# Which two slots of an attention stage carry no column block of the feed-forward matmul: third slots of a pair, or second ones

## The chip, the cores and the metric

One core of a Trainium2 chip runs the whole program. The metric is the device time of one execution in microseconds (us). The engines are named as in the profile: PE is TensorE, with PEld for its weight loads, DVE is VectorE, ACT is ScalarE, POOL is GpSimd, and SP is SyncE, which here only issues DMAs. Each engine takes its instructions in the order in which they stand in the program.

## The reference

Three layers follow each other: causal attention, a dense feed-forward layer, and a soft mixture of experts. Cut to what matters (q, k and v are 4 x 12 x 448 x 64, that is 4 batches of 12 heads; the middle layer is 768 to 2048 to 768 over 1792 tokens):

```python
scores = np.matmul(q, k.transpose(0, 1, 3, 2)) / np.sqrt(64)
attn = softmax(where(causal_mask, -1e9, scores))       # row maximum subtracted
x = (attn @ v).transpose(0, 2, 1, 3).reshape(1792, 768)
h = x @ w_in                                           # 768 -> 2048
g = np.maximum(0.01 * h, h)
x = g @ w_out                                          # 2048 -> 768
logits = x @ phi                                       # 32 slots, 4 for each of 8 experts
d, c = softmax(logits, axis=0), softmax(logits, axis=1)
slot_out[e] = np.maximum((d.T @ x)[e] @ w1[e], 0) @ w2[e]
out = c @ slot_out
```

## The kernel before, in words

Attention works on pairs of heads: there are 24, six for each batch. A generator, `attention_slots` (L506), hands out the work of a pair n in three slots. In the first slot PE multiplies the weights P of pair n-1 with v (tile O, from `attend`), transposes the maxima of pair n (mps), makes scores of pair n+1 for the row maxima (tile S_3, from `maxima`), and makes the first part of the transposed scores of pair n (T_0, from `weights`). The second slot makes the sums of pair n-1 (dn), the second part of the scores for the maxima (S_0) and T_1. The third slot turns pair n-1 into a piece of x16 (`columns`, no PE work from pair 6 on), and has T_2, S_1 and the eight transpositions of q and k of pair n+2 (qkps). So the names T_0, T_1, T_2 and S_3, S_0, S_1 say in which slot a tile stands.

ACT takes the exponential of every T (L397, to P); POOL clears the upper triangle of P (L401). DVE finds the maxima in every S by four instructions in the second slot (L361), and there it also takes two reciprocals of the sums (L439). The T and S tiles share two PSUM buffers, so that a T is written when the exponential of an older T, or the maxima of an older S, have been taken. H tiles have one PSUM buffer. Two buffers more (tag "tr") serve qkps, mps, dn and the small products.

The feed-forward layer is filled in between. The generator `up` (L585) gives for each of the 16 blocks of 128 columns of w_in one H of 18 matmuls, which take 3.5 us at full clock, followed by the activation g on ACT (L627). `stage` (L743) runs attention and `up` side by side: in slot x of 18 it issues the attention of the slot and then one H, except where x is in GAPS (L997), because there are 18 slots and 16 blocks. There are three such stages, for the batches 1, 2 and 3 of attention, beside `up(0)`, `up(1)` and `up(2)`. In the third, H is cut in two halves by the transposition of an older g (tile gps). A stage starts with the first slot of a pair, so that slots 8 and 17 are the third slots of the third and the sixth pair.

Also in between, in pieces that `prep_step` moves on after each slot, the weights w_in and w_out are converted from 64 to 32 bits: raw_i and raw_o are loaded, and ACT (L196, L197), DVE (L200, L201) and POOL (L216, L232) make cv_i and cv_o of them. PE has a part in it: w_ps, wt_ps, wp_ps and wf_ps. What stands with high priority (attention and `up`) keeps its order on PE by an explicit chain (L98); a scheduler places the rest around it.

After the stages, `up(3)` runs together with the logits of the older batches, while SP loads the experts' weights (w, L832) into buffers that become free.

Of the kernel before, what the change touches and what calls it, by code (L numbers as in the profile page):

```python
# [34 lines left out]
def tile_attn_moe_softmoe(ctx: ExitStack, tc: tile.TileContext, q, k, v, w_in, w_out, phi, w1, w2, out, dbg=None):  # L35
# [707 lines left out]
    def stage(slots, count, columns_of_g=None):  # L743

        had = started[0]
        for x in range(slots):
            with tc.high_priority(offset=AHEAD):
                next(slots_of_attention, None)
                if columns_of_g is not None and x not in GAPS:
                    next(columns_of_g)  # L750
# [243 lines left out]
NSPARE = 6  # L994
SPREAD = (1, 2)
VRING = 7
GAPS = (8, 17)  # L997


def tc_release(pool):  # L1000
# [31 lines left out]
```

## Time and profile before

| | |
|---|---|
| three timed runs | 711.86, 721.18, 721.48 us (median 721.18) |
| the profiled execution | 718.55 us; its span in the trace 716.8 us |
| busy: PE, DVE, ACT, POOL | 86%, 47%, 42%, 32% of the span |
| PE's H matmuls | 1152, busy 240.6 us |
| the three stages with GAPS | about 115 to 480 us from the span's start |

The profile lists the instructions of each engine in order of time, with the idle time ahead of each and the engine that ended it. Three timed runs lie up to 9.6 us apart, so a difference of a few microseconds between two executions says little.

### The profile page before, as it was taken

The page shows a single profiled execution, that of the slowest core. Times are in us where ns is not written, and L with a number is a line of the kernel's source. Part 1 is how long each engine was busy: PE and PEld are TensorE (multiplying, and loading weights), DVE is VectorE, ACT ScalarE, POOL GpSimd, SP SyncE. Part 2 cuts the span into 40 slices and gives each one's busy share as a digit, 9 for nine tenths or more (in the row PEclk, how much of TensorE's full clock was granted, in tenths as well). Part 3 has the DMA queues.
Part 4 walks back from the last instruction along what each step waited for, and adds up shares of the span by engine and source line. Part 5 has one row for each costly group of instructions (what it writes and reads, how often), then busy time and mean ns, then how long its engine had stood idle before and what let it go on. Part 6 is the DMA issues. An engine that isn't in the chain of part 4 may idle for free.

```text
span 716.8 us, 12198 instructions
## 1 busy us (share of the span) xinstructions
PE 616.6 (86%) x4764; PEld 350.0 (49%) x4764; DVE 338.9 (47%) x877; ACT 302.8 (42%) x596; POOL 231.5 (32%) x247
## 2 busy tenths in 40 slices
PE   3788859998978999899998999999999997984573
PEld 2455535554544555555555555554656553541121
DVE  5787645677875644563363555324334313010023
ACT  1677543566776545554445554422323220110012
POOL 4468733567765423442134442310000000000000
PEclk9799967999999999899999999999999999999877
DMA  9933154355345446422143222017759249999988
GB/s 196 250 95 78 39 173 139 109 166 152 102 157 197 122 132 206 134 84 74 53 127 115 67 67 68 23 52 276 262 198 333 83 177 350 408 400 399 393 287 270
DMA packets 117704, 125.66 MB, mean 175 GB/s; under 512 B 69520, under 2 KB 99216, under 8 KB 117648
## 3 DMA queue, kind: packets, MB, share of 16 engines
q1 hardware_dynamic: 117648, 124.90, 53.8%
q8 instruction: 37, 0.61, 0.3%
q14 instruction: 19, 0.16, 0.1%
HBM read 105.74 MB, written 19.14 MB: 174 GB/s over the span
## 4 chain that ended last, share of the span: by engine, by line
PE 55%; DMA 14%; DVE 12%; ACT 8%; POOL 3%; issue 3%; SPq 2%; DVEq 0%; ACTq 0%
PE H L100 24%; DMA w<-in_moe_w_dram 8%; PE O L100 6%; PE gps L100 4%; PE T L100 3%; DVE rs L439 2%; PE ph L897 2%; DMA v<-in_v_dram 2%; PE L L100 2%; PE pg L100 2%; DVE junk L361 2%; DMA raw_i_None<-in_moe_w_in_dram 2%; ACT mr L373 2%; PE qkps L100 2%; DMA raw_o<-in_moe_w_out_dram 2%
## 5 line engine op out<-in xcount | busy, mean ns | idle before, releaser
L100 PE MATMUL H<-x,w 128*128 128x448 f16 x1152 | 240.6, 354 | 1.5 <-ACT g L627 1.5
L100 PEld LDWEIGHTS <-w 128*128 128x128 f16 x1152 | 109.0, 98 | 103.7 <-issue 21.2
L361 DVE CUSTOM_DVE_ANT_0 junk<-S,mask 112x448 bf16<-112x448 f32 (+1 forms) x192 | 84.8, 442 | 74.5 <-PE S L100 72.0
L401 POOL TENSOR_SCALAR_AFFINE_SELECT P<-P 112x448 f32<-112x448 f32 x48 | 29.8, 621 | 144.3 <-ACT P L397 144.3
L627 ACT ACTIVATE g<-H,iv 128x448 f32<-128x448 f32 x58 | 36.6, 631 | 71.9 <-PE H L100 63.8
L397 ACT ACTIVATE P<-T 112x672 f32<-112x672 f32 (+1 forms) x72 | 57.0, 791 | 23.4 <-PE T L100 23.1
L100 PE MATMUL T<-qkt 64*112 64x336 f32 (+3 forms) x576 | 59.6, 319 | 6.1 <-ACT P L397 5.5
L100 PE MATMUL O<-P,v 112*64 112x448 f32 (+3 forms) x384 | 58.3, 449 | 5.0 <-POOL P L401 4.7
L439 DVE RECIPROCAL rs<-rs 128x224 f32<-128x224 f32 x36 | 53.3, 1521 | 12.6 <-ACT rs L437 12.6
L100 PEld LDWEIGHTS T<-qkt 64*112 64x112 f32 x576 | 45.4, 185 | 14.7 <-ACT P L397 6.9
L977 PE MATMUL po<-w,hz 128*32 128x384 f32 x256 | 30.3, 598 | 25.1 <-DMA w<-in_moe_w_dram 25.1
L410 POOL TENSOR_TENSOR tsum<-tsum,P 112x448 f32<-112x448 f32 (+1 forms) x48 | 44.8, 933 | 2.7
L100 PEld LDWEIGHTS O<-P,v 112*64 112x64 f32 x384 | 27.5, 150 | 34.8 <-issue 16.5
L373 ACT ACTIVATE mr<-mps,own 128x112 fp32r<-128x112 f32 x96 | 26.0, 354 | 43.2 <-PE mps L100 43.2
L570 DVE COPY g_nat<-gps 112x512 f32<-112x512 f32 x32 | 22.1, 689 | 44.1 <-PE gps L100 44.1
L568 ACT COPY g_nat<-gps 112x512 f32<-112x512 f32 x32 | 18.7, 584 | 54.3 <-PE gps L100 54.2
L406 POOL TENSOR_TENSOR tsum<-P 112x672 f32<-112x672 f32 x24 | 40.3, 1680 | 1.8
L100 PE MATMUL S<-qkt 64*112 64x448 f32 (+1 forms) x192 | 33.6, 391 | 7.1 <-DVE mxe L361 4.1
L100 PE MATMUL T<-mr,onesr 64*112 64x448 f32 (+1 forms) x192 | 32.0, 330 | 6.4 <-ACT mr L373 6.3
L890 POOL MEMSET hz<- 128x256 f32 x2 | 0.6, 311 | 112.8 <-PE pg L100 112.8
L216 POOL TENSOR_TENSOR cv_i_None<-cv_i_None,cs_i_None 128x768 f32<-128x768 f32 x16 | 26.8, 1681 | 28.6 <-ACT cs_i_None L215 28.5
L339 DVE TENSOR_TENSOR qkt<-qkps,qkt 128x448 fp32r<-128x448 f32 x48 | 28.1, 618 | 14.0 <-ACT qkt L338 14.0
(181 smaller groups left out, 898.8 us busy)
## 6 DMA issues: line engine op xcount, KB each, us to landing
w<-in_moe_w_dram SPq DMA_DIRECT2D x32, 1536.0 KB, 18.2
raw_i_None<-in_moe_w_in_dram SPq DMA_DIRECT2D x16, 768.0 KB, 5.9
raw_o_None<-in_moe_w_out_dram SPq DMA_DIRECT2D x10, 768.0 KB, 5.5
g_far<-g SPq DMA_DIRECT2D x32, 224.0 KB, 2.0
gb<-g_far SPq DMA_DIRECT2D x8, 896.0 KB, 8.5
wo<-wsc SPq DMA_DIRECT2D x4, 1536.0 KB, 6.4
qk<-in_q_dram SPq DMA_DIRECT2D x48, 112.0 KB, 2.6
qk<-in_k_dram SPq DMA_DIRECT2D x48, 112.0 KB, 2.9
```

The source lines that it names most:

```text
L100: op(*args, **kwargs)
L216: nc.gpsimd.tensor_tensor(t, t, sg, ALU.mult)
L339: nc.vector.tensor_tensor(st[:, j, 1], p, st[:, j, 0].bitcast(F32), ALU.subtract)
L361: nc.vector.tensor_tensor_reduce(out=junk[:, :w], in0=ps[:, a, at : at + w], in1=mask[:, S - w :], scale=-1.0, scalar=3e38, op0=ALU.add, o ...
L373: nc.scalar.activation(mr[:, i], ps, AF.Copy, scale=own[:, i : i + 1])
L397: nc.scalar.activation(x[:, :, o : o + at], ps[:, :, :at], AF.Exp, scale=SCALE)
L401: nc.gpsimd.affine_select(out=d, in_=d, compare_op=ALU.is_ge, fill=0.0, base=0, pattern=[[0, 4], [1, CP]], channel_multiplier=-1,)
L406: nc.gpsimd.tensor_tensor(tsum[:CP], p[0][:CP, :, 0, CP:], p[0][:CP, :, 1, : S - CP], ALU.add)
L410: nc.gpsimd.tensor_tensor(y, y, p[1][:CP, :, j, : S - CP * (j + 2)], ALU.add)
L439: nc.vector.reciprocal(rs[:, c : c + S // 2], rs[:, c : c + S // 2])
L627: nc.scalar.activation(g, ps, AF.Prelu, scale=iv[b][:, f : f + 1], alpha=SLOPE)
L977: nc.tensor.matmul(po[h][32 * g : 32 * g + 32], hp[:, (t0 + t) % 8], wt[:, t, DH * h - c0 : DH * (h + 1) - c0], start=t0 + t < 4, stop=t0 ...
```

## The change

One table changes: the slots of a stage that get no H.

```diff
-GAPS = (8, 17)
+GAPS = (7, 16)
```

Before, slots 8 and 17 had none. Now slots 7 and 16 have none, which are the second slots of the same pairs. Slot 7's block moves to slot 8, and slot 16's to slot 17; all other blocks stay. This makes six places. In the last of them (the end of the third stage) attention has no PE work left in the third slot, and the order on PE is as before. The other five are called A and B (first stage, pairs 9 and 12), C and D (second stage, pairs 15 and 18) and E (third stage, pair 21). In each, the H that stood between T_1 and T_2 now stands between qkps and O.

At C, PE's order was this before. In the names, T15_1 and T15_2 are the second and the third part of the transposed scores of pair 15, S16_1 is the last part of the scores of pair 16, qkps17 are the transpositions of pair 17; in brackets stand the semaphores that a row waits for.

```order
L100 MATMUL T15_1_3280<-mr15_3200,onesr_121 112x336 x2
L100 MATMUL H1_7_3292<-x16_1_1493,w16_1_99 128x448
...
L100 MATMUL wp_ps3_3314<-wt3_3247,phi_sb_93 32x128 [waits Activation_49]
L100 MATMUL wt_ps4_1_3329<-ident_64,cv_o4_None_3179 128x128 [waits Activation_49]
L100 MATMUL T15_2_3347<-qkt15_2859 112x224 x6
L100 MATMUL S16_1_3368<-qkt16_3122 112x224 [waits DVE_49]
L100 MATMUL qkps17_1_3383<-ident_64,qk17_2874 128x112 [waits DMAHW7_49,DMAHW6_49,Activation_49]
L100 MATMUL wf_ps3_3398<-istack_69,w4_3_3321 128x32 [waits DVE_49]
L100 MATMUL O15_3420<-P1_448_147,v15_2023 64x448 [waits Pool_49]
```

And this is the same place now.

```order
L100 MATMUL T15_1_3280<-mr15_3200,onesr_121 112x336 x2
L100 MATMUL wp_ps3_3292<-wt3_3247,phi_sb_93 32x128 [waits Activation_49]
L100 MATMUL wt_ps4_1_3307<-ident_64,cv_o4_None_3179 128x128 [waits Activation_49]
L100 MATMUL T15_2_3325<-qkt15_2859 112x224 x6
L100 MATMUL S16_1_3346<-qkt16_3122 112x224 [waits Activation_49]
L100 MATMUL qkps17_1_3361<-ident_64,qk17_2874 128x112 [waits DMAHW7_49,DMAHW6_49]
L100 MATMUL H1_7_3376<-x16_1_1493,w16_1_99 128x448
...
L100 MATMUL wf_ps3_3398<-istack_69,w4_3_3299 128x32 [waits DVE_49]
L100 MATMUL O15_3420<-P1_448_147,v15_2000 64x448 [waits Pool_49]
```

H1_7 moved from behind T15_1 to behind qkps17, and S16_1 now waits for ACT where it waited for DVE: it got the PSUM buffer of T15_2, and so waits for the exponential of T15_2 just ahead of it. This is so at B, C, D and E; at A it still waits for DVE, as before.

At B, where PE has nothing else between the two T, its order before was (T12 and mr12 belong to pair 12, S13 to pair 13):

```order
L100 MATMUL T12_1_2594<-mr12_2527,onesr_121 112x336 x2
L100 MATMUL H0_15_2607<-x16_0_500,w16_3_101 128x448 [waits Activation_49]
...
L100 MATMUL T12_2_2632<-qkt12_2232 112x224 [waits Activation_49]
L100 MATMUL S13_1_2653<-qkt13_2470 112x224 [waits DVE_49]
L100 MATMUL qkps14_0_2661<-ident_64,qk14_2247 128x112 [waits DMAHW6_49,DMAHW5_49]
L100 MATMUL O12_2694<-P0_448_145,v12_1314 64x448 [waits Pool_49]
```

Now it is:

```order
L100 MATMUL T12_1_2594<-mr12_2527,onesr_121 112x336 x2
L100 MATMUL T12_2_2609<-qkt12_2232 112x224 [waits Activation_49]
L100 MATMUL S13_1_2630<-qkt13_2470 112x224 [waits Activation_49]
L100 MATMUL qkps14_0_2638<-ident_64,qk14_2247 128x112 [waits DMAHW6_49,DMAHW5_49]
L100 MATMUL H0_15_2672<-x16_0_500,w16_3_101 128x448
...
L100 MATMUL O12_2694<-P0_448_145,v12_1314 64x448 [waits DVE_49,Pool_49]
```

T12_2 follows T12_1 at once, and waits for the exponential of T12_1, whose PSUM buffer it takes, as it did before with H0_15 in between.

At D, the order on ACT changes as well. Before (qkt20 is the copy of qkps20, mr19 the lowered maxima that PE needs for the last step of T_0 of pair 19, raw_o10 a block of w_out that is loaded at the start of the third stage):

```order
L338 CAST qkt20_4078<-qkps20_1_4086 128x448 [waits PE_49]
L373 ACTIVATE mr19_4134<-mps19_4132,own_124 128x112 [waits PE_49,Activation_49]
L397 ACTIVATE P1_448_147<-T19_0_4146 112x2x448 [waits PE_49]
L196 ACTIVATE cv_o10_0_4179<-raw_o10_0_4118 128x384 [waits DMAHW1_49]
L197 ACTIVATE cs_o10_0_4180<-raw_o10_0_4118 128x384
L196 ACTIVATE cv_o10_1_4250<-raw_o10_1_4120 128x384 [waits DMAHW2_49]
```

Now:

```order
L338 CAST qkt20_4056<-qkps20_1_4064 128x448 [waits PE_49]
L627 ACTIVATE g1_15_4107<-H1_15_4088,iv1_2727 128x448 [waits DMAHW5_49,PE_49]
L196 ACTIVATE cv_o10_0_4179<-raw_o10_0_4118 128x384 [waits DMAHW0_49]
L197 ACTIVATE cs_o10_0_4180<-raw_o10_0_4118 128x384
L196 ACTIVATE cv_o10_1_4250<-raw_o10_1_4120 128x384 [waits DMAHW1_49]
L373 ACTIVATE mr19_4134<-mps19_4132,own_124 128x112 [waits PE_49,Activation_49]
```

The conversions of raw_o10, which wait for its load, moved ahead of mr19.

## Rows read from the trace of the kernel before

**Rows 1.** The page: span, and busy time and instructions of each engine.

```profile
span 716.8 us, 12198 instructions
PE 616.6 (86%) x4764; PEld 350.0 (49%) x4764; DVE 338.9 (47%) x877; ACT 302.8 (42%) x596; POOL 231.5 (32%) x247
```

**Rows 2.** Waits of SP's queue: line waited for, us in total, times, longest.

```profile
SPq L832 <- PE H L100: 42.1, 4, 20.7
```

**Rows 3.** Timeline of PE, a regular pair; columns: start, us, instructions, count [idle before].

```profile
247.77 0.57 PE L100 MATMUL T<-qkt 64*112 64x224 f32 x6
...
249.79 3.57 PE L100 MATMUL H<-x,w 128*128 128x448 f16 x18
...
253.94 2.11 PE L100 MATMUL O<-P,v 112*64 112x448 f32 x16
...
257.86 3.58 PE L100 MATMUL H<-x,w 128*128 128x448 f16 x18
```

**Rows 4.** Timeline of PE at A: end of T_1, the wait, next H.

```profile
164.30 0.32 PE L100 MATMUL T<-mr,onesr 64*112 64x336 f32 x2
...
174.60 0.60 PE L111 MATMUL w_ps<-ident,w_am 128*128 128x128 f32 x2 [2.90 <-DVE qkt L339]
...
179.27 3.58 PE L100 MATMUL H<-x,w 128*128 128x448 f16 x18
```

**Rows 5.** Timeline of PE at C: end of T_1, the wait, O, next H.

```profile
287.77 0.32 PE L100 MATMUL T<-mr,onesr 64*112 64x336 f32 x2
...
297.66 0.61 PE L100 MATMUL wf_ps<-istack,w 96*128 96x32 f32 x2 [2.50 <-DVE qkt L339]
...
299.20 4.00 PE L100 MATMUL O<-P,v 112*64 112x448 f32 x16
...
305.18 3.58 PE L100 MATMUL H<-x,w 128*128 128x448 f16 x18
```

**Rows 6.** Timeline of PE at B: end of T_1, next H but one.

```profile
228.67 0.32 PE L100 MATMUL T<-mr,onesr 64*112 64x336 f32 x2
...
238.79 3.58 PE L100 MATMUL H<-x,w 128*128 128x448 f16 x18
```

**Rows 7.** Timeline of PE at D: end of T_1, next H but one.

```profile
356.52 0.32 PE L100 MATMUL T<-mr,onesr 64*112 64x336 f32 x2
...
366.68 3.58 PE L100 MATMUL H<-x,w 128*128 128x448 f16 x18
```

**Rows 8.** Timeline of PE at E: end of T_1, next H but one (first half).

```profile
420.61 0.32 PE L100 MATMUL T<-mr,onesr 64*112 64x336 f32 x2
...
433.34 1.88 PE L100 MATMUL H<-x,w 128*128 128x448 f16 x9
```

**Rows 9.** Timeline of ACT at A, B, C, D and E.

```profile
166.45 0.72 ACT L397 ACTIVATE P<-T 112x672 f32<-112x672 f32 x1
...
229.80 0.71 ACT L397 ACTIVATE P<-T 112x672 f32<-112x672 f32 x1
...
294.05 0.94 ACT L196 ACTIVATE cv_o_None<-raw_o_None 128x768 f32<-128x768 f32 x1
...
365.15 1.09 ACT L373 ACTIVATE mr<-mps,own 128x112 fp32r<-128x112 f32 x4 [2.03 <-PE mps L100]
...
369.94 0.55 ACT L196 ACTIVATE cv_o<-raw_o 128x384 f32<-128x384 f32 x1 [2.04 <-DMA raw_o<-in_moe_w_out_dram]
...
423.90 0.55 ACT L197 ACTIVATE cs_o<-raw_o 128x384 bf16<-128x384 f32 x1 [2.21 <-DMA raw_o<-in_moe_w_out_dram]
```

**Rows 10.** Three stretches: length, busy us of each engine, granted clock, DMA.

```profile
211.00:216.00 5.00, 2.88 (x20) 1.93 (x21) 4.93 (x15) 2.86 (x6) 4.11 (x3) 1.00 0.39 142
298.00:304.00 6.00, 6.00 (x33) 3.06 (x34) 0.13 (x1) 1.62 (x5) 2.56 (x3) 0.50 0.51 149
376.00:384.00 8.00, 6.37 (x44) 4.09 (x43) 4.63 (x16) 4.98 (x10) 5.67 (x6) 0.79 0.42 119
```

## The prediction

> **What bounds the kernel now.** I read the page first: PE is busy 616.6 us of a span of 716.8 us, and no other engine more than 49% [rows 1]. So in the stages PE is the engine to follow, and a microsecond in which PE stands still there is one that the end gets. It reaches the end undiminished: the weights of the experts are loaded when PE's last H tiles have freed their buffers (SP's queue waits for PE's H 42.1 us in four waits [rows 2]), so that the tail, where DMA is the bound, starts when PE gets there.
>
> Then I read PE's timeline at the five places, always from the end of T_1 to the H that follows O, because between these two points the change moves one H and nothing leaves. The reader is to see what each neighbour of H hides. Before, the two old waits in slot 8 stand out: at A PE waits 2.90 us [rows 4] and at C 2.50 us [rows 5], both behind qkps, for DVE's copy of qkt, because the small product after qkps needs the buffer that DVE still reads. [...] At B, D and E PE has no such wait, or a short one.
>
> **The change, part by part.** Nothing is added or removed: the same instructions run, one H of 3.5 us moves in each of five places. What it covered is laid open, and what stands behind it now is covered.
>
> *What is laid open.* T_2 takes the PSUM buffer of T_1, so it cannot start before ACT has taken the exponential of T_1. Before, H ran in that time. S_1 waits at B, C, D and E for the exponential of T_2 right ahead of it, a wait that did not exist. An exponential takes 0.71 to 0.72 us [rows 9] once ACT comes to it; T_2 itself has about 0.9 us.
>
> *What is covered.* The 3.5 us of H now lie over DVE's copies of qkt and over POOL's work on P. The waits at A and C should be gone.
>
> *Unit for the sum.* In a regular pair T_2 to H is 2.02 us, H to the next is 3.5, and O to the H after it is 3.92 (257.86 - 253.94) [rows 3]; together 9.4 us at full clock. Each place then is: its waits, its small products, and 9.4.
>
> A. Before: 164.62 to 179.27, 14.65 us [rows 4]. ACT ended the exponential of T_1 at 166.45 + 0.72 = 167.17, since conversions of w_in stood ahead of it [rows 9]. So T_2 starts 2.6 us late. S_1 waits for DVE's maxima, which come behind its reciprocals: between nothing and 0.9 us (the price of the new wait at the other places), I take 0.45. With two w_ps of 0.35 each: 2.6 + 0.45 + 9.4 + 0.7 = 13.15. Gain 1.5 us.
>
> C. Before: 288.09 to 305.18, 17.1 us [rows 5]. Now wp_ps and wt_ps stand between T_1 and T_2, 1.6 us of work which covers the exponential. Behind T_2, ACT has a conversion of 0.94 us [rows 9] to do ahead of the exponential, so S_1 waits 1.2 us. Then wf_ps and wp_ps, 0.8: 1.6 + 1.2 + 9.4 + 0.8 = 13.0. Gain 4.1 us, of which the clock is the larger part: O to H took 5.98 us there [rows 5] instead of 3.92.
>
> B. Before: 228.99 to 238.79, 9.8 us [rows 6]. The exponential of T_1 started at 229.80 [rows 9], behind a conversion that had waited for its load; it ends at 230.51, so T_2 is 1.6 us late. S_1 waits 0.9 for its exponential. With one v_ps of 0.3: 1.6 + 0.9 + 9.4 + 0.3 = 12.2. Loss 2.4 us.
>
> D. Before: 356.84 to 366.68, 9.84 us [rows 7]. The same pair of waits, with ACT taken as idle: 0.65 and 0.85; 1.5 + 9.4 + 0.4 = 11.3, loss 1.5 us. But on ACT four conversions of raw_o10 now stand ahead of mr19, without which PE cannot end T_0 of pair 19. They started at 369.94, when the load had landed [rows 9]. The loads follow the transpositions qkps20, which now end some 1.85 us earlier (3.5 us of H gone, 1.5 us of waits and handing over come), so the conversions start between 368.1 and 369.9 and need 1.9 us (four of nearly 0.5); mr19 takes 1.09 [rows 9], and H follows 0.4 later: 371.5 to 373.3 instead of the 368.1 without the block. The loss is thus 1.5 us at least (load early, no block) and 6.6 at most; I take 4. Something comes back: before, the same loads held up PE in the first slots of the third stage, 1.6 us of idle time and a mean clock of 0.79 in 376 to 384 [rows 10], which is 1.6 + 8 x 0.21 = 3.3 us. With the loads early and PE late these should mostly go; I take 3 of them. D comes to a loss of 1.
>
> E. Before: 420.93 to 433.34, 12.4 us [rows 8]. T_2 waits 0.3 behind wp_ps. The exponential of T_2 stands on ACT behind a conversion that ran at 423.90, when its load landed, to 424.45 [rows 9]. T_2 ends at about 422.6, so S_1 starts only at 425.2, 2.55 us late. With gps, wf_ps and wt_ps: 0.6 + 0.3 + 2.55 + 9.4 + 1.1 = 13.95. Loss 1.5 us.
>
> Sum at full clock: +1.5 + 4.1 - 2.4 - 1 - 1.5 = 0.7 us gained.
>
> *The clock.* It is the term that the trace leaves open. After 2.50 us of idle PE at C the granted clock fell; after 2.1 us of idle (5.00 - 2.88) at 211 to 216 it stayed at 1.00 [rows 10]; in 376 to 384 1.6 us in two pieces let it fall. A fall costs between 1.7 us (8 x 0.21 [rows 10]) and 2.8 us (at C: 2.06 from O to H, and 0.7 in the small products ahead of O [rows 5, 3]). New idle times are 3.05 at A, 2.5 at B, 1.2 at C, 1.5 or more at D, 2.85 at E, each in two pieces close together. I count two falls of 1.7: 3.4 us, though none or four are as well possible.
>
> [...]
>
> Forecast: -0.7 + 3.4 = 2.7 us slower. On the profiled execution, 718.55 us, that is 721.3. The median of the three runs, 721.18, lies 2.6 us above that execution, and the lowest, 711.86, lies 6.7 below; I set 722 us for the median, between 721.3 and 723.9.
>
> **The rivals.**
>
> 1. *The new waits are hidden.* ACT could come to the exponentials earlier, because g has left its place ahead of them; then T_2 and S_1 wait only 0.7 each. For it: at D and E g did stand in that stretch. Against: at A and B what stood ahead were conversions and their loads, which stay. Priced: A, B and E gain another 1.5 us each, no clock falls: -0.7 - 4.5 = 5 us faster, 713.3 on the profiled execution, 716 by the median.
>
> [...]
>
> 3. *Slower by more: D's block without the return.* ACT stands on the load of raw_o10 while PE runs out of work, its loads are not earlier, and the old holdup in 376 to 384 stays: loss of 6.6 at D in place of 1, with a fall of the clock of 2.8 and two more falls of 1.7. The sum is -0.7 + 5.6 + 6.2 = 11 us, 730 to 733 us; it becomes more than 2% (14.4 us) only if the gain at C fails too, 735 us and more. It decides once the conversions start after 369.9.
>
> 4. *Nothing moves where it matters.* At the sixth place the order on PE is the same, so nothing changes there; for the other five the order shows the move, which leaves this rival no room of its own.
>
> **How the numbers follow.** Forecast within 5 us of 722: 0.6. Rival 1: 0.17. Rival 2: 0.13. Rival 3: 0.1, of which 0.03 go beyond 2%. The likeliest is 722. Low: rival 1 on an execution like the lowest of the three would be 707; leaving that out, 712 takes in its 716 and the spread below. High: 731, which takes in most of rival 2. So 712 to 731 us; the forecast's own range is 717 to 727. What a measurement of this kernel can tell from no change is about 2%, 14.4 us: faster 0.02, same 0.94, slower 0.04.
>
> **What would show it.** In the profile after: no wait for DVE's qkt of more than 1 us behind qkps at A and C, with the clock at 1.00 in the 10 us behind C, and O of 2.1 us there; T_2 waits for ACT's P at A and B by more than 1 us; S_1 waits for ACT's P at B, C, D, E by 0.8 to 2.6 us; mr19 late at D, with PE waiting for it, and no wait for wt in the slots after it. The total is wrong if the clock falls at none or at all of the places, or if the conversions, whose loads run on their own time, meet the exponentials otherwise than in this one execution. C is the largest single term: if its wait only moves to another place, the change is slower by 6 us or more.

## The result and the profile after

The changed kernel takes 728.66 us (median of four runs, 725.35 to 734.95), the kernel before 719.49 us beside it (four runs, 711.86 to 721.48). The ratio is 1.0147, with a 95% interval of 1.0098 to 1.0196, so the change costs 10.6 us (7 to 14). The forecast was a loss of 2.7 us, 722 us, with a range of 712 to 731: the sign was right and the size a quarter of what came. The time lies outside the forecast's own range (717 to 727), and inside the stated one only because that made room for rival 2, a clock fall at each of A, B, D and E (729 to 732), just below which it ended.

The page of the kernel after: span, busy time of each engine, and the granted clock in 40 equal slices, in tenths.

```profile
span 733.2 us, 12197 instructions
PE 623.5 (85%) x4764; PEld 353.7 (48%) x4764; DVE 344.7 (47%) x877; ACT 302.4 (41%) x596; POOL 231.7 (32%) x247
PEclk9999977998988799999999999999999998999787
```

The engines do the same work as before [rows 1]; PE is busy 6.9 us longer and idle 9.5 us longer. Ahead of a T it waits 11.5 us in all for ACT's P (5.5 before), ahead of an S 10.1 us for DVE's maxima (4.1 before). What the stages lose reaches the end, as the prediction assumed: the last O starts 15.4 us later (488.88 against 473.52), and the span is 16.4 us longer.

PE's timeline after shows the end of T_1, the waits and the H matmuls at the five places and, ahead of B, in pair 11 (columns as in [rows 3]). The first four rows are of A (before: [rows 4]), the next two of pair 11, then five of B ([rows 6]), four of C ([rows 5]), five of D ([rows 7]) and four of E ([rows 8]).

```profile
166.02 0.32 PE L100 MATMUL T<-mr,onesr 64*112 64x336 f32 x2
168.84 0.90 PE L100 MATMUL T<-qkt 64*112 64x224 f32 x6 [2.51 <-ACT P L397]
172.34 5.12 PE L100 MATMUL H<-x,w 128*128 128x448 f16 x18
181.75 0.55 PE L100 MATMUL H<-x,w 128*128 128x448 f16 x2
...
219.08 0.53 PE L100 MATMUL S<-qkt 64*112 64x224 f32 x2 [4.28 <-DVE mxe L361]
221.09 4.65 PE L100 MATMUL H<-x,w 128*128 128x448 f16 x18
...
234.82 0.32 PE L100 MATMUL T<-mr,onesr 64*112 64x336 f32 x2
238.77 0.91 PE L100 MATMUL T<-qkt 64*112 64x224 f32 x6 [3.64 <-ACT P L397]
241.34 0.53 PE L100 MATMUL S<-qkt 64*112 64x224 f32 x2 [0.82 <-ACT P L397]
243.34 5.46 PE L100 MATMUL H<-x,w 128*128 128x448 f16 x18
252.98 3.58 PE L100 MATMUL H<-x,w 128*128 128x448 f16 x18
...
301.97 0.32 PE L100 MATMUL T<-mr,onesr 64*112 64x336 f32 x2
305.82 0.36 PE L100 MATMUL S<-qkt 64*112 64x224 f32 x2 [1.04 <-ACT P L397]
311.66 0.41 PE L100 MATMUL wf_ps<-istack,w 96*128 96x32 f32 x2 [1.16 <-DVE qkt L339]
316.68 3.58 PE L100 MATMUL H<-x,w 128*128 128x448 f16 x18
...
368.01 0.32 PE L100 MATMUL T<-mr,onesr 64*112 64x336 f32 x2
369.15 0.56 PE L100 MATMUL T<-qkt 64*112 64x224 f32 x6 [0.49 <-ACT P L397]
370.99 0.36 PE L100 MATMUL S<-qkt 64*112 64x224 f32 x2 [0.82 <-ACT P L397]
381.58 0.45 PE L100 MATMUL T<-mr,onesr 64*112 64x448 f32 x2 [2.36 <-ACT mr L373]
381.97 3.58 PE L100 MATMUL H<-x,w 128*128 128x448 f16 x18
...
433.04 0.32 PE L100 MATMUL T<-mr,onesr 64*112 64x336 f32 x2
437.58 0.36 PE L100 MATMUL S<-qkt 64*112 64x224 f32 x2 [2.38 <-ACT P L397]
439.03 3.20 PE L100 MATMUL H<-x,w 128*128 128x448 f16 x9
448.73 1.88 PE L100 MATMUL H<-x,w 128*128 128x448 f16 x9
```

Nearly every wait that the prediction named is there (only S_1 at A has none): T_2 and S_1 wait for ACT's P, and an H of 3.6 us behind such a wait takes up to 5.46 us. From the end of T_1 to the H behind O, A takes 15.41 us (before 14.65), B 17.84 (9.8), C 14.39 (17.1), D 13.64 (9.84), E 15.37 (12.4). The windows (length, busy time of PE, PEld, DVE, ACT, POOL, then the granted clock, DMA) show where the clock fell:

```profile
170.00:182.00 12.00, 12.00 (x69) 6.94 (x68) 8.55 (x18) 5.70 (x13) 7.49 (x6) 0.77 0.67 197
236.00:249.00 13.00, 9.41 (x46) 5.80 (x48) 5.87 (x15) 3.91 (x7) 5.51 (x6) 0.61 0.21 57
300.00:318.00 18.00, 15.49 (x133) 9.20 (x132) 12.62 (x26) 11.31 (x23) 9.74 (x8) 1.00 0.50 152
368.00:384.00 16.00, 12.33 (x92) 7.17 (x89) 10.40 (x30) 8.16 (x18) 7.48 (x8) 1.00 0.49 137
436.00:446.00 10.00, 8.42 (x45) 5.07 (x47) 4.64 (x15) 4.23 (x9) 3.85 (x5) 0.83 0.03 12
```

These are A, B, C, D and E: the clock fell at A, B and E, and stayed at 1.00 at C and D. It fell in pair 11 too, twice: H took 5.21 us in its first slot (at 202.86; the clock was 0.76 in 202 to 209) and 4.65 in its third (the row at 221.09; 0.65 in 217 to 226).

One stretch that the prediction did not look at lost time as well. Against the profile of before, O of pair 10 starts 2.5 us later (196.47 against 193.98), and O of pair 11 7.9 us later (225.67 against 217.74): 5.4 us are lost in between, where the change moves nothing on PE.

### The profile page after: what moved, and what is told of

It reads as the page before. It is cut to its first block, busy times and chain, and to the rows that moved or that the text cites. A ratio compares the mean times of both kernels' runs of the same rounds, so it can differ in the third digit from the quotient of the medians.

```text
span 733.2 us, 12197 instructions
## 1 busy us (share of the span) xinstructions
PE 623.5 (85%) x4764; PEld 353.7 (48%) x4764; DVE 344.7 (47%) x877; ACT 302.4 (41%) x596; POOL 231.7 (32%) x247
## 5 line engine op out<-in xcount | busy, mean ns | idle before, releaser
L100 PE MATMUL H<-x,w 128*128 128x448 f16 x1152 | 246.8, 361 | 1.3 <-ACT g L627 1.3
L100 PEld LDWEIGHTS <-w 128*128 128x128 f16 x1152 | 111.3, 100 | 106.6 <-issue 27.0
L100 PE MATMUL T<-qkt 64*112 64x336 f32 (+3 forms) x576 | 60.3, 322 | 12.2 <-ACT P L397 11.5
L100 PE MATMUL O<-P,v 112*64 112x448 f32 (+3 forms) x384 | 53.7, 422 | 5.1 <-POOL P L401 4.7
L410 POOL TENSOR_TENSOR tsum<-tsum,P 112x448 f32<-112x448 f32 (+1 forms) x48 | 46.7, 972 | 2.2
L100 PE MATMUL S<-qkt 64*112 64x448 f32 (+1 forms) x192 | 33.4, 388 | 15.7 <-DVE mxe L361 10.1
L100 PEld LDWEIGHTS O<-P,v 112*64 112x64 f32 x384 | 26.1, 141 | 33.2 <-issue 16.4
L406 POOL TENSOR_TENSOR tsum<-P 112x672 f32<-112x672 f32 x24 | 39.8, 1660 | 1.7
```

The costliest lines, as they stand in the source:

```text
L100: op(*args, **kwargs)
L406: nc.gpsimd.tensor_tensor(tsum[:CP], p[0][:CP, :, 0, CP:], p[0][:CP, :, 1, : S - CP], ALU.add)
L410: nc.gpsimd.tensor_tensor(y, y, p[1][:CP, :, j, : S - CP * (j + 2)], ALU.add)
```

## The experiments

The theory was that each place costs its new buffer waits and the clock fall behind them, and that the rest (pair 11, and B's T_2 wait of 3.64) follows from A. The rivals were a clock fall at every moved place alike, and spread between executions. The kernels run the same instructions in another order; e6_b_raw4 and e7_raw4 have one buffer more, and e8_b_fill adds matmuls that nothing reads.

**Parts of the change.** GAPS becomes a table by stage, `x not in GAPS[b]`:

```diff
-GAPS = (8, 17)
+GAPS = (7, 17)                                  # e1_pair1: A, C, E
+GAPS = (8, 16)                                  # e2_pair2: B, D
+GAPS = {1: (7, 16), 2: (8, 17), 3: (8, 17)}     # e3_stage1: A, B
+GAPS = {1: (8, 17), 2: (7, 17), 3: (8, 17)}     # e4_c_alone: C
+GAPS = {1: (8, 16), 2: (8, 17), 3: (8, 17)}     # e5_b_alone: B
```

> Only the first of the two slots moves (7, 17): places A (stage 1), C (stage 2) and E (stage 3). Theory (each place costs what its new buffer waits and the clock fall behind them cost, as the trace of the changed kernel shows it place by place): A -0.8, C +2.7, E -3.0, so 1 us slower than before, within 0.5%. Rival 1 (the 5.4 us lost between A and B is a knock-on of A): 6 to 7 us slower, 0.9%, and the stretch between H_8 and H_15 shows it again. Rival 2 (every moved place costs a clock fall of 1.7 us and nothing else): 5 us slower at all three places alike.

> Only the second of the two slots moves (8, 16): places B (stage 1) and D (stage 2). Theory: B -6.3 and D -0.9, 7 us slower than before, 1.0%, with a wait of T_2 of over 3 us and a clock of 0.50 at B. Rival 1 (B lost so much only because the pairs ahead of it were late and a load of w_in then stood ahead of the exponential on ScalarE): B costs 2 to 3 us, the kernel is 3 to 4 us slower. Rival 2 (a clock fall of 1.7 us at each place): 3.4 us slower.

> Stage 1 alone gets the new slots (places A and B). Theory: A -0.8, the stretch between A and B -5.4, B -6.3: 12 us slower than before, more than the whole change cost by its median (9.2), since C gives 2.7 back. Rival 1 (the stretch between A and B is spread between executions): 7 us slower. Rival 2 (two clock falls): 3.4 us slower.

> Place C alone (first slot of stage 2). Theory: the wait of 2.50 us and the slow matrix products behind it go, a wait of S_1 of about 1.0 us comes: 2.7 us faster than before, 0.4%, and faster than both kernels. Rival (a moved place costs a clock fall wherever it is): 1.7 us slower.

> Place B alone (second slot of pair 12 in stage 1). Theory: B is where the change loses most, and loses more than the 2.4 us of the sum: 6 to 7 us slower than before (0.9%), of which e2_pair2 showed 4.9 in its trace and the changed kernel 6.3. T_2 waits over 1 us for ACT's P, and the granted clock falls to 0.50 in the H behind. Rival 1 (the prediction's own price, 2.4 and a clock fall of 1.7): 4.1 us slower. Rival 2 (D carries the loss of e2_pair2): within 2 us of before.

| | ratio to before, 95% interval | us |
|---|---|---|
| e1_pair1 (A, C, E) | 1.0024 [0.9997, 1.0051] | +1.7 |
| e2_pair2 (B, D) | 1.0121 [1.0083, 1.0159] | +8.7 |
| e3_stage1 (A, B) | 1.0108 [1.0064, 1.0151] | +7.8 |
| e4_c_alone (C) | 0.9982 [0.9955, 1.0008] | -1.3 |
| e5_b_alone (B) | 1.0068 [1.0039, 1.0098] | +4.9 |

The us are the ratio less 1, times 720; each is uncertain by 2 to 3 us either way, and a difference of two of them by 3 to 4. The parts add up: e1_pair1 and e2_pair2 give 10.4, the whole change 10.6. B costs 4.9, D the other 3.8 of e2_pair2. C gives 1.3, half of what the theory had from one trace, and its interval includes nothing as well as the 2.7 of the theory. A and E with pair 11 cost about 3 together (1.7 + 1.3). That a moved place costs one fall of 1.7 us wherever it is, falls with e2_pair2 (8.7 where it said 3.4) and e4_c_alone. The theory missed as well: e3_stage1 costs 7.8 where it said 12, e5_b_alone 4.9 where it said 6 to 7 (the prediction's own price, 4.1, fits too), and the loss of e2_pair2 is not 6.3 at B and 0.9 at D, as the next table shows.

The traces say more, place by place. (The profiled execution of e3_stage1 was the longest of its six, 736.64 us.) The table gives the us from the start of T_1 to the first H behind O (for pair 11 from O of pair 10 to its own O), each from two rows of PE's timeline; a star marks a place with the new slot.

| | A | pair 11 | B | C | D | pair 19, behind D | E |
|---|---|---|---|---|---|---|---|
| before | 15.43 | 23.76 | 10.58 | 17.87 | 10.63 | 18.51 | 13.20 |
| e10_before_again | 16.80 | 24.11 | 10.58 | 17.88 | 10.64 | 16.85 | 13.20 |
| after | 16.19* | 29.20 | 18.63* | 15.17* | 14.42* | 15.63 | 16.15* |
| e11_after_again | 16.71* | 29.56 | 18.93* | 15.18* | 14.72* | 15.59 | 16.27* |
| e1_pair1 | 17.00* | 28.90 | 12.19 | 15.16* | 10.62 | 16.27 | 16.03* |
| e2_pair2 | 15.29 | 23.51 | 13.97* | 15.35 | 14.44* | 15.94 | 13.19 |
| e3_stage1 | 16.89* | 31.64 | 16.71* | 17.86 | 10.63 | 18.49 | 14.89 |
| e4_c_alone | 16.84 | 23.51 | 10.58 | 15.47* | 10.63 | 16.15 | 13.19 |
| e5_b_alone | 16.53 | 24.32 | 14.09* | 15.34 | 10.63 | 16.77 | 13.20 |
| e6_b_raw4 | 14.59 | 24.33 | 14.42* | 17.85 | 10.63 | 16.01 | 13.20 |
| e7_raw4 | 16.25 | 24.35 | 10.94 | 15.36 | 10.63 | 16.47 | 13.20 |
| e8_b_fill | 15.77 | 24.34 | 13.99* | 17.87 | 10.62 | 16.77 | 17.01 |

D and E cost about 3.8 and 2.9 wherever they are moved, and D nothing where it is not; E, unmoved, loses 1.7 us in e3_stage1 by the clock alone (O takes 3.80 us) and 3.8 in e8_b_fill, for which see below. B costs 3.4 to 3.8 with A unmoved, and 6.1 to 8.4 with A moved; even unmoved, behind a moved A, it loses 1.6 (e1_pair1). Pair 11 loses 4.5 us and more in each of the four traces with A moved, and in none of the eight others. C is the surprise: left as it was, it takes 17.9 us in some traces and 15.4 in others.

**The clock at C.** The next rows are of PE at C in e2_pair2, then in e6_b_raw4; in neither does the change touch C.

```profile
305.37 0.41 PE L100 MATMUL wf_ps<-istack,w 96*128 96x32 f32 x2 [2.50 <-DVE qkt L339]
306.46 2.11 PE L100 MATMUL O<-P,v 112*64 112x448 f32 x16
```

```profile
301.29 0.63 PE L100 MATMUL wf_ps<-istack,w 96*128 96x32 f32 x2 [2.49 <-DVE qkt L339]
302.86 4.00 PE L100 MATMUL O<-P,v 112*64 112x448 f32 x16
```

The wait is the same, and the work ahead of it too. In one O takes 2.11 us, in the other 4.00. Of the eight traces with C unmoved, e2_pair2, e5_b_alone and e7_raw4 kept the clock (O 2.11 us in each); before (twice), e3_stage1, e6_b_raw4 and e8_b_fill lost it (4.00 in each). So 2.5 of the 2.7 us that the trace of the changed kernel gains at C are the clock (17.87 against 15.34 to 15.36 with C unmoved), and are there to be gained only in an execution in which it had fallen behind the wait.

**Both kernels once more**, nothing edited.

> The kernel before, profiled once more, nothing changed. Theory (the clock falls after one and the same wait in one execution and not in another): the places A to E wait as in the first profile, 2.9 at A, 2.5 at C and none over 0.5 at B and D, but the stretch at C can take 15.4 instead of 17.9 us, the one behind D 16 to 17 instead of 18.5, and the first slot of pair 12 can lose the clock where it did not. Rival (the clock follows from the program): every stretch within 0.3 us of the first profile.

> The changed kernel, profiled once more, nothing changed. Theory: the waits come again (T_2 2.5 to 3.7 at A and over 1 at B, S_1 0.8 at B and D, 2.4 at E), B with A moved ahead of it takes 16 to 19 us where B alone took 14.1, D 14.4, E 16.1; only the stretches of pair 11 and A vary, by 1 to 2 us, as the clock falls or not. Rival (the loss between A and B of the first profile was an accident of that execution): pair 11 takes no longer than in the kernel before.

In the kernel before, C lost the clock again (17.88), which the theory had left open; behind D the stretch took 16.85 in place of 18.51, and pair 12 kept the clock (H 3.58 us at 226.43). So it is not the program alone that decides, but the two traces agree in more than I expected. In the changed kernel pair 11 took 29.56, so its loss is no accident. S_1 there waited 5.95 us for DVE, and T_2 at B 3.93 us for ACT.

Here one program shows both outcomes of the clock. Behind the same two waits for qkt, of 0.8 and 1.4 us, the H in the first slot of pair 11 took 5.21 us in the first profile and 3.58 in the second (at 202.96). The pair is no shorter for it: S_1 waits 1.7 us longer for DVE and starts at the same time (219.22 against 219.08). So a clock fall ahead of a longer wait cost nothing here.

**What B costs: the load, or the two exponentials?** Four buffers for the loaded blocks, with B alone and without it.

```diff
-    BUFS = ((3, 4, 2), (3, 3, 2), (2, 2, 2))
+    BUFS = ((3, 4, 2), (4, 3, 2), (2, 2, 2))
```

> B alone, and four buffers instead of three for the loaded blocks of w_in and w_out in the first two stages with H, so that the block of w_out that ACT converts ahead of the exponential of T_1 at B can be loaded earlier. To be compared with e7_raw4. Theory (the load, which ACT waits for ahead of the exponential, makes B dear): at B no wait of ACT for raw_o ahead of the exponential, T_2 waits under 1.5 us, and this is 2.5 to 4 us slower than e7_raw4. Rival (two exponentials in a row and the clock fall alone make B dear, whenever the load comes): 6 to 7 us slower than e7_raw4.

> The kernel before with four buffers for the loaded blocks instead of three, to compare e6_b_raw4 with. Theory: loads come earlier, and the waits of ACT for raw blocks that hold up mr or the exponentials in stages 1 and 2 get shorter: 1 to 4 us faster than before. Rival (the loads are bound by the conversions that free the buffers): same within 1 us.

e7_raw4 has a ratio of 1.0002 (0.9977 to 1.0027), e6_b_raw4 one of 1.0015 (0.9986 to 1.0044). The difference is 0.9 us with some 2.8 either way: the rival's price of 6 to 7 is out, but what makes up B's cost the times don't tell. The traces do for the place: with the load taken earlier (no conversion stands between g and the exponential any more), T_2 still waits 1.32 and S_1 0.83 us, and B takes 3.5 us more than in e7_raw4, as in e5_b_alone against before. So in its place B alone does not cost what it costs because of the load; two exponentials in a row and the clock do it. By the times B costs 0.9 us with four buffers and 4.9 with three, 4.0 apart with some 3.5 either way; where the rest went is open. PE at B in e5_b_alone:

```profile
235.25 0.57 PE L100 MATMUL T<-qkt 64*112 64x224 f32 x6 [0.99 <-ACT P L397]
237.09 0.49 PE L100 MATMUL S<-qkt 64*112 64x224 f32 x2 [0.82 <-ACT P L397]
239.06 4.33 PE L100 MATMUL H<-x,w 128*128 128x448 f16 x18
```

T_2 to H takes 3.81 us, of which 0.82 are the wait and 2.02 the work at full clock [rows 3]; the 0.97 left and the 0.75 that H takes beyond 3.58 are the clock: 1.7 us.

**Filling the waits.** B alone, with matmuls that nothing reads in the place of the waits.

```diff
+    def fill(count):
+        ps = psum.tile([128, S], F32, tag="H", bufs=HB[0], name=f"fill{count}")
+        for step in range(count):
+            mm(ps, w16[3][:, 0, 0, :128], x16[0][:, 0, 0, :], start=step == 0, stop=step == count - 1)
...
                 weights(n, 1)
+            if n == 12:
+                fill(9)
             yield
...
                 weights(n, 2)
+            if n == 12:
+                fill(4)
```

> B alone, with 9 extra matmuls of H's kind (1.8 us) into H's free buffer between T_1 and T_2, and 4 (0.8 us) between T_2 and S_1; nothing reads their results. They only keep PE at work while it would wait. Theory (the fall of the clock is a good part of what B costs): the H of slot 17 takes 3.6 us instead of 4.2 to 5.5, the granted clock stays at 1.00, and in spite of 2.6 us more work the kernel is 1 to 2.5 us faster than e5_b_alone. Rival (the waits themselves are the whole cost): no faster than e5_b_alone, up to 1 us slower.

PE at B in e8_b_fill:

```profile
233.15 1.88 PE L100 MATMUL fill<-x,w 128*128 128x448 f16 x9
235.90 0.93 PE L100 MATMUL fill<-x,w 128*128 128x448 f16 x4
...
238.67 3.57 PE L100 MATMUL H<-x,w 128*128 128x448 f16 x18
```

And a window over B in e5_b_alone, then in e8_b_fill:

```profile
233.00:243.00 10.00, 8.19 (x57) 5.36 (x56) 6.69 (x17) 4.30 (x7) 5.50 (x6) 0.83 0.26 69
```

```profile
232.00:242.00 10.00, 9.27 (x71) 5.48 (x69) 6.79 (x17) 4.10 (x7) 5.56 (x6) 1.00 0.24 64
```

The clock stays at 1.00, H takes 3.57 us, and 2.8 us of extra work cost nothing in the place: B takes 13.99 us, with e5_b_alone at 14.09. So by these two traces the fall at B comes with PE standing still there, and its size, half of B's cost, fits; that filling makes the kernel faster does not hold. The kernel as a whole took 1.0166 (1.0127 to 1.0205), 7 us more than e5_b_alone. In its trace 2.5 us are the clock at C (17.87 against 15.34), and the larger loss is at E, which the edit was not to touch: 17.01 us in place of 13.20, with a wait of PE for mr of 3.75 us and a clock fall behind it. What changed there is the order on ACT, as at D: a conversion of raw_o that waits for its load stands ahead of mr. ACT at E in e8_b_fill:

```profile
440.81 0.54 ACT L197 ACTIVATE cs_o<-raw_o 128x384 bf16<-128x384 f32 x1 [4.42 <-DMA raw_o<-in_moe_w_out_dram]
441.26 1.06 ACT L373 ACTIVATE mr<-mps,own 128x112 fp32r<-128x112 f32 x4
```

In the kernel before mr ran first (431.81), and the conversion behind it (435.03); there and in e5_b_alone PE waited under 0.2 us for mr. So the fill at B cost its gain by a new order somewhere else.

**The first slots.** What if the slot without H is one whose H covers little?

```diff
-GAPS = (8, 17)
+GAPS = (6, 15)     # e9_first
+GAPS = (6, 17)     # e12_first_third
```

> The first slots of the same pairs carry no H (6, 15). Then the H between T_1 and T_2 stays, and one stands between qkps and O too; what is laid open is the exponential of T_0 (0.92 us), over which the dn products and S_0 (1.6 us in the kernel before, pair 9) run. Theory (a slot is worth what its H covers): T_1 waits for nothing or under 0.5 us, no place costs more than 0.5 us, the waits for DVE's qkt of 2.90 at A and 2.50 at C go, with the clock falls behind them where they came: 3 to 7 us faster than before, 0.4 to 1.0%. Rival (any slot without H lays a wait open and brings a clock fall): 5 to 10 us slower, like the changed kernel.

> In each stage the first slot of the third pair and, as in the kernel before, the third slot of the sixth pair carry no H (6, 17). By the traces the first slot is cheap at A, C and E, while at B and D the third slot is the cheapest: with no H in the first slot of pair 18 (15) e9_first waited 2.19 us for mr there, behind the conversions of raw_o10, and took 64.0 us from O of pair 17 to O of pair 20 where kernels with D as before took 61.3 to 63.7. Theory: the gains of e9_first at A and C stay, its losses at B (0.7) and D (0.3 to 2.7) go: 5 to 8 us faster than before, 0.7 to 1.1%, and 1 to 3 us faster than e9_first. Rival (the gains of e9_first come from the second of its slots): no faster than before.

e9_first takes 718.78 us (ratio 0.9939, 0.9911 to 0.9968; 4.4 us faster), e12_first_third 712.82 us (0.9882, 0.9838 to 0.9926; 8.5 us faster than before). The first time came as expected (3 to 7; at D it still waits 2.19 us for mr), the second a little beyond its range (5 to 8), and both kernels beat the two compared here. Windows over A and C in e12_first_third:

```profile
159.00:174.00 15.00, 12.58 (x92) 7.09 (x92) 12.20 (x35) 10.64 (x17) 9.52 (x8) 1.00 0.44 115
289.00:299.00 10.00, 9.53 (x80) 5.75 (x77) 4.88 (x16) 6.88 (x16) 5.70 (x6) 1.00 0.83 260
```

No wait for qkt of 2.9 or 2.5 us is left at A and C, as H stands behind qkps there, and H also stands between T_1 and T_2. What is laid open, the exponential of T_0, costs under 0.5 us, because dn and S_0 run over it. A still has 2.11 us of waiting (S_1 for DVE's maxima), without a fall of the clock. Against the first trace of before the gain lies at C, 4.8 us (2.5 of them the clock that this trace had lost), in pairs 9 to 11 together, 2.4 (pair 10 loses 3.6 by a wait of S_1 and a clock fall, pair 11 gains 4.4), and behind D, 2.3; E gains nothing.

## Why the prediction came out as it did

**The waits at the places: right.** T_2 waits 2.51 us at A (2.6 in the sum), 0.49 at D (0.65), 0.26 at E (0.3); S_1 waits 1.04 at C (1.2), 0.82 at B and D (0.9, 0.85), 2.38 at E (2.55). Three did not come so: S_1 at A has no wait (0.45 in the sum), T_2 at B waits 3.64 us (1.6; 0.99 with B alone), and wf_ps at C still 1.16 (nothing). At D the conversions of raw_o10 stand ahead of mr19 as the order said. ACT at D, after:

```profile
378.55 0.55 ACT L196 ACTIVATE cv_o<-raw_o 128x384 f32<-128x384 f32 x1 [2.21 <-DMA raw_o<-in_moe_w_out_dram]
...
380.47 1.07 ACT L373 ACTIVATE mr<-mps,own 128x112 fp32r<-128x112 f32 x4
```

PE waits 2.36 us for mr, and D loses 3.8 us, where I took 4 between bounds of 1.5 and 6.6. That it came so close is in part luck: with T_1 at D 11.49 us later than before (368.01 against 356.52), the conversions started 1.0 us ahead of the earliest time that the sum had allowed (378.55 - 11.49 is 367.06, not 368.1). From 368.1 the sum gives a loss of 4.8, from 367.06 the 3.8 that came. So rival 1 (waits hidden) and rival 3 (conversions after 369.9) are both out.

**The clock: the number of falls was wrong.** I counted two falls of 1.7 us. It fell at A, B and E: 3.0 us at A (T_2 to H is 3.50 in place of 2.02, and H to O 5.05 in place of 3.5), 1.7 at B alone and 3.6 with A moved (T_2 to H 3.75 without the wait, and H 5.46), 1.7 at E (3.20 for half an H in place of 1.88, and qkps 1.38 in place of 0.99). At full clock A would have gained the 1.5 us of the sum and 0.7 more; with the fall it lost 0.8 (and in other traces A unmoved takes from 14.6 to 16.8 us where the first took 15.4, by the clock and by a wait of H for g of up to 1.7 us). These falls, 8.3 us in place of 3.4, are, with the 5.4 us of pair 11 below, the largest parts of the miss in the trace. Rival 2's term, four falls at up to 2.8 us each, no run shows: the traces have three, at A, B and E, of 3.0, 3.6 and 1.7 us, while D waited 0.49, 0.82 and 2.36 us with the clock at 1.00. That the total came out near its 10.5 us is therefore partly luck: it had nothing in pair 11.

**Three returns were booked against one execution.** At A the sum gave a gain of 1.5 us. But the trace of before had lost the clock there too, behind the wait of 2.90 us, which the prediction did not see:

```profile
174.00:180.00 6.00, 5.40 (x27) 3.19 (x28) 4.70 (x14) 1.71 (x5) 1.94 (x3) 0.72 0.58 169
```

That is 1.7 us (6 x 0.28), so the gain is no more than that execution's own loss; behind the same wait (2.90 and 2.91 us) e2_pair2 and e6_b_raw4 kept the clock (O's second part 0.79 us, 1.39 in that trace). At C I took 4.1 us, the larger part for the clock that the first trace had lost there; in three of the eight traces with C unmoved it had not been lost. The wait did not go away either: S_1's 1.04 came as priced, but wf_ps still waits 1.16 us for DVE's qkt, behind H, which the sum had at nothing. C alone gives 1.3 us by the times (between a loss of 0.6 and a gain of 3.2), 2.4 by its trace against both of before; how often the kernel before loses the clock at C is open, since both of its traces did. At D I took 3 of 3.3 us back from the slots behind it. In the profile of before these took 18.51 us, and 15.63 after, so by that trace the 3 came; but in the other traces with D unmoved they take 16.0 to 16.9, except e3_stage1 (18.49). D as a whole cost 3.8 us by the times, not 1.

**Pair 11 was not looked at: the queue that was moved past.** The loss there follows A (four traces of four, none of eight without). Two things changed. First, S_1 of pair 11 now gets the PSUM buffer of S_0, and so waits for DVE's maxima; before, it had that of T_2 and waited for ACT, 2.24 us. Second, SP's queue is in another order: the load of v for pair 17 comes behind two blocks of w_out instead of between them. SP after (start, us, instruction, count; the second issue waits within the 4.80 us):

```profile
198.47 4.80 SPq L173 DMA_DIRECT2D raw_o_None<-in_moe_w_out_dram  x2
...
204.38 0.38 SPq L311 DMA_DIRECT2D v<-in_v_dram  x1
```

The same place in e10_before_again:

```profile
198.07 0.35 SPq L173 DMA_DIRECT2D raw_o_None<-in_moe_w_out_dram  x1
...
198.99 0.38 SPq L311 DMA_DIRECT2D v<-in_v_dram  x1
204.73 0.33 SPq L173 DMA_DIRECT2D raw_o_None<-in_moe_w_out_dram  x1
```

DVE after: its instruction for that v stands ahead of the maxima of S_0 that PE waits for, and a conversion too.

```profile
209.53 0.69 DVE L324 TENSOR_REDUCE v_am<-v 112x1 f32<-112x512 f32 x1 [3.49 <-DMA v<-in_v_dram]
...
214.33 2.92 DVE L200 TENSOR_SCALAR cv_o_None<-cv_o_None 128x768 int32<-128x768 int32 x1
```

Both changes stand in the order of the program; the prediction followed PE and ACT and left SP, DVE and the pairs between the places out. Which of them costs how much wasn't tried. An estimate: in e10_before_again, where O of pair 10 starts 0.1 us later, DVE had done with these maxima at 217.98 and S_1, waiting for ACT, started at 216.10; in the changed kernel it started at 219.08. So of some 3.1 us the buffer by itself would make 1.9 and the late maxima the rest; the clock fall behind S_1 adds 2.0 (qkps 1.75 us, H 4.65). In e12_first_third, with the S_0 buffer and the old order of SP, v was reduced at 201.51 and pair 11 has no such wait; but there DVE takes the maxima ahead of a conversion as well, so this is no clean test.

**What B costs beside A.** At B the sum had 2.4 us, and 4.1 with a fall. B alone cost 4.9 us by the times, 3.5 in its trace: right in size. With A moved its T_2 waits 3.64 us, since ACT waits for a block of w_out ahead of the exponential. ACT after:

```profile
237.22 0.88 ACT L197 ACTIVATE cs_o_None<-raw_o_None 128x768 bf16<-128x768 f32 x1 [2.07 <-DMA raw_o_None<-in_moe_w_out_dram]
238.01 0.71 ACT L397 ACTIVATE P<-T 112x672 f32<-112x672 f32 x1
```

In the kernel before, PE had waited 1.97 us for mr in the first slot of pair 12, because a conversion stood ahead of mr on ACT (221.15 and 221.95); now mr runs first (228.06), and PE waits 0.18. But SP issues the two blocks of w_out no sooner behind O of pair 11 (2.6 us, 3.0 before), so PE meets their load at T_2: by this 1.8 of the 8.0 us are only moved.

**What stays open.** The profiled executions with A moved lie above the medians of the same kernels (e1_pair1 3.1 us, e3_stage1 6.7, the changed kernel 6.3 and 7.6), those of the kernels with A unmoved from 3.7 below to 0.5 above. So the timed executions seem to pay less at pair 11 and B than the traces show. By the times A and pair 11 cost 2.9 us together (e3_stage1 less e5_b_alone), with some 3.8 either way. Why, no run shows.

By the times the sum is then: B 4.9, D 3.8, A with pair 11 and E 3.0, less 1.3 at C, 10.4 us. A, pair 11 and E have no time of their own; how their 3.0 us divide is known from traces only.

## What to carry to other kernels

Before moving work from one place to another, list what it covers at both places and choose the place where other work already covers the wait: here two first slots were worth 4 us, a first and a third one 8, and two second slots cost 10, with the same instructions. Follow the move through every queue and up to the next pair, not only on the engine that bounds the kernel, since here a load of v that came behind one more block in SP's queue was reduced on DVE 4.4 us later (209.53 against 205.11 in e10_before_again), ahead of maxima that PE waited for. A gain that rests on a clock fall or a holdup seen in one trace should be counted by how often it comes, so look for it in a second trace of the same kernel, and in traces of its neighbours.

## What the hardware showed

One and the same wait of 2.5 us at C, with the same rows ahead of it, was followed by different granted clocks: O took 4.00 us in the kernel before (0.50 in 298 to 304, [rows 10]) and 2.11 in e2_pair2 (1.00 in 304 to 310). In pair 11 of the changed kernel even one program had both, in two executions (H 5.21 and 3.58 us). The falls at A, B and E cost from 1.7 to 3.6 us. With thirteen matmuls without use (1.88 and 0.93 us) where two waits had been, the clock over B was 1.00 in e8_b_fill, and 0.83 in e5_b_alone without them; they cost nothing in that place (13.99 against 14.09 us).

DVE's conversion L200 took 2.92 us at 214.33 in the changed kernel, while POOL's L406 and L474 ran from 214.23 to 216.82, which is 0.4 us ahead of the end of the conversion. In the kernel before it took 0.74 us at 210.51, with POOL's L406 beginning behind it (210.92), and in e10_before_again 0.75 us at 213.48. That POOL's work made it longer was not shown: no run moved one of the two alone.
